# Second MLP of a three-stage kernel: out2's matmuls in rows of four instead of six, and one product of val moved on VectorE

## The chip, the cores and the metric

The kernel runs on one core of one Trainium2 chip, as one launch. The metric is the device time of that launch in microseconds (us), the median of several runs; less is better. The core has the engines TensorE (PE for matmuls, PEld for the weight loads that go ahead of them), VectorE (DVE), ScalarE (ACT) and GpSimd (POOL), and SyncE (SP), from which the transfers are started.

## What is computed

The reference computes an attention whose scores are masked by hash buckets, and two MLPs behind it. The second MLP, on 1536 tokens with a width of 512 and a hidden width of 1536, is what the change touches:

```python
def _moe2_ref(x, w_gate, w_val, w_out):
    g = x @ w_gate
    silu = g * (1.0 / (1.0 + np.exp(-g)))
    val = x @ w_val
    return (silu * val @ w_out).astype(np.float32)
```

## The kernel before

All matmuls run in fp32r with every operand split into a high and a low part, and a product is three matmuls: high x high, high x low, low x high (`each_of_three`, L802).

The second MLP runs in twelve steps, m = 0 to 11: two halves of the tokens (768 each) times six pairs of chunks of the hidden width. A step has a gate group and a val group (`group`, L1125) and is followed by its share of out2, which the next step carries. A group forms a 256 x 768 block by a scheme of seven half-size products in place of eight. Each of the seven is six matmuls of 384 columns into a PSUM bank; here they are named by bank and product: X1, Y6, X2, Y7, Z5, Y4, Z3, in this order. There are two banks only. X and Z share one, Y is the other, and the next group takes them the other way round: its X lies where this group's Y was, its Y where this group's Z was.

Between the products DVE and ACT read the banks. The ACT copies X1 to p1 (L1156). DVE forms u2 = p1 + Y6 (L1148); the next product into that bank, Y7, can't start before DVE has read it. In the same way u3 = p1 + Y7 stands ahead of Y4, the sum of Z5 ahead of Z3, the sum of Y4 ahead of the next group's X1, and the sum of Z3, which is the group's last addition, ahead of the next group's Y6. The four results are the quarters "11", "22", "21", "12".

In a gate group each quarter goes through Silu on ACT (tile sg, L1097). In a val group each quarter is multiplied by sg on DVE (L1103, `gating`, tile u), then copied by ACT to its high part uh (L1108), and DVE forms the low part ul = u - uh (L1109, both in `two`). Three of the four products read one operand from PSUM; that of "22" reads two SBUF tiles (val and sg). It is not issued at once but put on a list, `later`, and so is every `two`. `settle(n)` issues the first n entries of that list. So `settle` decides where on the queues of DVE and ACT these stand, and both engines work through their queues in order.

out2 of step m is 36 matmuls of 512 columns (tile o): the quarters in the order "11", "22", "21", "12", nine matmuls each. They need uh and ul of their quarter. They are handed out by a generator, `filler`, a few at each of the seven places `rest(0)` to `rest(6)` behind the products of the next step's groups. `counts` says how many at each place; before the change steps 2 to 11 have (6, 0, 6, 0, 6, 0, 0) in gate and (0, 6, 0, 6, 0, 6, 0) in val. out2 of the last step, m = 11, has no groups behind it and runs at the end in the order "11", "21", "22", "12".

`prepare` (L1035) makes the weight pieces of the coming group out of two loaded chunks: sums and differences x and y on DVE (L1057 to L1064, two SBUF operands each), high parts on ACT and low parts on POOL (L1030, L1031, tiles gate_t and val_t). `chores(k)` puts a part of it behind each product. In steps 1 to 5 `token_sums` for the second half of the tokens runs there too (L979, L987, L1004, L1006), and in step 6 the first half's results are copied out of PSUM (L1241, L1243, tile ot). The fill of the list by step is the same on every engine: the order is written out by hand, and no planner moves it.

Of the kernel before, what the change touches and what calls it, by code (L numbers as in the profile page):

```python
# [27 lines left out]
def lsh_attention_moe_moe2(  # L28
# [1096 lines left out]
    def group(nm, m, filler, counts, chores):  # L1125


        g = 2 * m + (nm == "val")
        sb, p = divmod(m, NPP)
        (pa, ta), (pb, tb_) = banks[g % 2], banks[1 - g % 2]  # L1130
        w = pieces.pop((nm, m))
        rights = {
            i: (quarter(xh, kh, th, sb), quarter(xl, kh, th, sb))
            for i, kh, th in ((1, 0, 0), (2, 1, 0), (3, 1, 1))
        }
        def temp(what):
            return pools["right"].tile([P, HALF], F32, tag="w", bufs=NR, name=f"{nm}{m}{what}")

        def mm(bank, i, first):
            right = rights[i] if i < 4 else sums_of_x[sb, {4: 3, 5: 0, 6: 1, 7: 2}[i]]  # L1140
            product(bank, w[i], right, first)

        def rest(k):
            for _ in range(counts[k]):
                next(filler, None)

        def add(out, a, bank):
            nc.vector.tensor_tensor(out=out, in0=bank[:, :HALF], in1=a, op=ALU.add)  # L1148
            return out

        X = pa.tile([P, 512], F32, tag=ta, name=f"{nm}{m}X")
        Y = pb.tile([P, 512], F32, tag=tb_, name=f"{nm}{m}Y")
        mm(X, 1, True)
        rest(0)
        p1 = temp("p1")
        nc.scalar.activation(out=p1, in_=X[:, :HALF], func=AF.Copy)  # L1156
        settle(2)
        late = nm == "gate" and m in (0, NPP)
        if not late:
            chores(0)  # L1160
        mm(Y, 6, True)
        rest(1)
        u2 = add(temp("u2"), p1, Y)
        if late:
            chores(0)
        chores(1)
        mm(X, 2, False)
        rest(2)
        take(nm, m, "11", X[:, :HALF])
        chores(2)  # L1170
        mm(Y, 7, False)
        rest(3)
        u3 = add(temp("u3"), p1, Y)
        settle(1)
        chores(3)
        Z = pa.tile([P, 512], F32, tag=ta, name=f"{nm}{m}Z")
        mm(Z, 5, True)
        rest(4)
        take(nm, m, "22", add(temp("22"), u3, Z))
        chores(4)  # L1180
        mm(Y, 4, False)
        rest(5)
        take(nm, m, "21", add(temp("21") if nm == "gate" else Y[:, :HALF], p1, Y))
        settle(1)
        chores(5)
        mm(Z, 3, False)
        rest(6)
        take(nm, m, "12", add(temp("12") if nm == "gate" else Z[:, :HALF], u2, Z))
        settle(1)
        chores(6)  # L1190

    out_v = out.rearrange("(b p c) d -> b c p d", b=B, c=NBLK)
# [119 lines left out]
    for m in range(NSTEP):  # L1312
        if m == 0:
            ahead = out2(0)
            filler = itertools.chain(out1(N1 - 2), out1(N1 - 1), ahead)
        else:
            filler = ahead if m == 1 else out2(m - 1)
        if m == 1:
            tsum = token_sums(
                1,  # L1320
                lambda i, name: (early if i % 2 else pools["late"]).tile(
                    [P, 2, HALF], F32, tag="raw", bufs=2, name=name
                ),
            )
        for nm in ("gate", "val"):
            nxt = ("val", m) if nm == "gate" else ("gate", m + 1)
            after = ("gate", m + 1) if nm == "gate" else ("val", m + 1)
            ready = prepare(*nxt)

            def chores(k):  # L1330
                if k == 0:
                    fetch_group(*after)
                next(ready, None)
                rows = {("val", 0, 0): [0], ("val", 0, 2): [1], ("val", 0, 3): [2], ("val", 0, 5): [3]}
                out1_close(N1 - 1, rows.get((nm, m, k), []))
                if nm == "gate" and k == 3:
                    fetch2("out2", m, 0)
                    fetch2("out2", m, 1)
                if nm == "val" and k in (1, 3):
                    prepare_out(m, 0 if k == 1 else 1)  # L1340
                if 1 <= m < 5 and k in (2, 5):
                    next(tsum, None)
                if m == NPP - 1 and nm == "val" and k in (2, 4, 5, 6):
                    next(tsum, None)

            if m == 0:
                counts = (2, 2, 2, 2, 2, 3, 3) if nm == "gate" else (2, 2, 2, 2, 0, 2, 2)
            elif m == 1 and nm == "gate":
                counts = (6, 0, 4, 0, 4, 0, 0)
            else:  # L1350
                counts = (6, 0, 6, 0, 6, 0, 0) if nm == "gate" else (0, 6, 0, 6, 0, 6, 0)
            group(nm, m, filler, counts, chores)
            for _ in ready:
                pass
        for _ in filler if m else ():
            pass
# [34 lines left out]
```

## Time and profile before

| | |
|---|---|
| median of 3 runs | 770.41 us (770.36 to 770.46) |
| the profiled execution | 770.41 us, span 768.5 us |
| PE busy | 761.5 us (99%), 4107 matmuls |
| PEld busy | 640.1 us (83%) |
| DVE busy | 547.9 us (71%) |
| ACT busy | 520.8 us (68%) |
| POOL busy | 487.2 us (63%) |
| the chain that ended last | PE 97%, ACT 1%, DVE 1% |
| second MLP's steps | from about 481 us to 764 us |

The page gives busy time by engine and the chain of work that ended last, followed back from the last instruction. A matmul's record starts when it starts, and its end is modelled and reaches over the start of the next one; so the pace is read from the starts, and a stall from a start that comes late or from a wait of PEld, which loads the weights just ahead. Where the timeline merges equal instructions, the row gives the first start, the time to the last end, and the count.

### The profile page before, as it was taken

How to read it: one execution, taken by the hardware profiler on the slowest of the kernel's cores; microseconds unless marked ns; L12 is line 12 of the kernel's file. 1: busy time of each engine (PE TensorE's matmuls, PEld its weight loads, DVE VectorE, ACT ScalarE, POOL GpSimd, SP SyncE). 2: the span in 40 equal slices, each digit the busy share in tenths (PEclk: the TensorE clock that was granted, in tenths of full speed). 3: DMA queues.
4: the chain of work that ended last, by engine and by line, in shares of the span. 5: the costliest groups of instructions: out<-in, count | busy, mean ns of one | idle time of the engine just before them, and what ended most of it. 6: DMA issues, size and time to landing. Idle time of an engine off the chain costs nothing.

```text
span 768.5 us, 12675 instructions
## 1 busy us (share of the span) xinstructions
PE 761.5 (99%) x4107; PEld 640.1 (83%) x4107; DVE 547.9 (71%) x1092; ACT 520.8 (68%) x1020; POOL 487.2 (63%) x424
## 2 busy tenths in 40 slices
PE   8999999999999999999999999999999999999998
PEld 5777868777777888888888888999999999999996
DVE  7777778777755787766666798587776787665553
ACT  7778887988878788887788777653444454444433
POOL 5647555554556776777778988666665595656450
PEclk9999999999999999999999999999999999999999
DMA  7577576757115777688866755122222215221102
GB/s 217 135 180 165 164 191 150 202 164 179 56 55 174 243 261 255 205 309 285 280 186 217 239 175 185 42 70 82 70 54 72 69 27 205 70 82 43 42 1 83
DMA packets 72692, 113.01 MB, mean 147 GB/s; under 512 B 6675, under 2 KB 44979, under 8 KB 72627
## 3 DMA queue, kind: packets, MB, share of 16 engines
q1 hardware_dynamic: 72352, 112.08, 48.7%
q8 instruction: 33, 0.54, 0.3%
q14 instruction: 33, 0.26, 0.1%
q10 hardware_dynamic: 274, 0.13, 0.1%
HBM read 76.29 MB, written 18.35 MB: 123 GB/s over the span
## 4 chain that ended last, share of the span: by engine, by line
PE 97%; ACT 1%; DVE 1%; issue 0%; POOL 0%; DVEq 0%
PE o L804 30%; PE h L804 17%; PE av L618 8%; PE t L600 8%; PE s L540 4%; PE s L543 4%; PE pj L341 1%; PE trk L285 1%; PE trq L285 1%; ACT p L561 1%; PE gate6Y L804 0%; PE gate7Y L804 0%; PE gate0Y L804 0%; PE val6Y L804 0%; PE val5Y L804 0%; PE val2Y L804 0%
## 5 line engine op out<-in xcount | busy, mean ns | idle before, releaser
L579 POOL TENSOR_SCALAR p<-p,rv 128x768 f32<-128x768 f32 x96 | 89.0, 944 | 68.3 <-DVE rv L572 61.6
L550 DVE TENSOR_SCALAR_CACHE_REDUCE p<-s 128x768 f32<-128x768 f32 x96 | 91.5, 955 | 26.7 <-PE s L543 10.6
L561 ACT ACTIVATE p<-p,mn 128x768 f32<-128x768 f32 x96 | 89.0, 934 | 2.9 <-DVE p L550 2.7
L606 ACT ACTIVATE pt<-t 128x384 f32<-128x384 f32 x140 | 63.9, 488 | 23.8 <-PE t L600 23.6
L600 PE MATMUL t<-ident,p 128*128 128x128 f32 x576 | 79.1, 274 | 0.6 <-POOL p L579 0.5
L600 PEld LDWEIGHTS t<-ident,p 128*128 128x128 f32 x576 | 66.8, 140 | 13.6 <-POOL p L579 6.2
L618 PE MATMUL av<-pt,vn 128*64 128x384 f32 x384 | 66.0, 491 | 0.0
L1108 ACT ACTIVATE uh<-u 128x384 fp32r<-128x384 f32 x48 | 23.8, 521 | 59.1 <-DVE u L1103 59.1
L835 DVE SCALAR_TENSOR_TENSOR rf<-ki,h 128x512 f32<-128x512 int32 x47 | 32.7, 696 | 39.3 <-ACT ki L832 39.3
L540 PE MATMUL s<-Y,X 128*128 128x384 f32 x192 | 57.6, 381 | 0.5 <-DVE p L550 0.3
L618 PEld LDWEIGHTS av<-pt,vn 128*64 128x64 f32 x384 | 26.2, 137 | 34.9 <-issue 34.7
L847 ACT ACTIVATE r<-r 128x512 f32<-128x512 f32 x48 | 30.3, 632 | 31.1 <-DVE r L839 30.9
L859 DVE TENSOR_TENSOR g<-h,r 128x512 f32<-128x512 f32 x48 | 33.0, 687 | 24.6 <-ACT r L848 24.0
L543 PE MATMUL s<-W,Z 76*128 76x384 f32 x192 | 49.4, 339 | 0.7 <-DVE Z L469 0.5
L1097 ACT ACTIVATE sg<-gate 128x384 f32<-128x384 f32 x36 | 18.9, 525 | 43.0 <-DVE gate L1148 42.9
L139 ACT ACTIVATE w<-raw 128x512 f32<-128x512 f32 x68 | 44.9, 662 | 2.0 <-DMA raw<-in_moe_w_in_dram 2.0
L804 PE MATMUL o<-out_1s,uh 128*128 128x512 f32 x144 | 45.0, 392 | 0.0
L804 PE MATMUL o<-out_0s,uh 128*128 128x512 f32 x142 | 44.3, 392 | 0.0
L155 DVE TENSOR_SCALAR bw<-w 128x512 int32<-128x512 int32 x55 | 37.8, 688 | 3.2 <-ACT w L139 2.0
L832 ACT ACTIVATE ki<-h 128x512 int32<-128x512 f32 x48 | 28.3, 590 | 14.9 <-PE h L804 14.8
L160 DVE SCALAR_TENSOR_TENSOR w<-raw,bw 128x512 int32<-128x512 int32 x55 | 37.3, 679 | 0.3
L848 ACT ACTIVATE r<-r,halfpi 128x512 f32<-128x512 f32 x48 | 34.8, 725 | 1.5
(1824 smaller groups left out, 2389.4 us busy)
## 6 DMA issues: line engine op xcount, KB each, us to landing
f<-w SPq DMA_DIRECT2D x58, 256.0 KB
raw<-in_moe_w_out_dram SPq DMA_DIRECT2D x28, 512.0 KB
raw<-in_moe_w_in_dram SPq DMA_DIRECT2D x16, 512.0 KB
raw<-in_moe_w_gate_dram SPq DMA_DIRECT2D x12, 512.0 KB
raw<-in_moe_w_val_dram SPq DMA_DIRECT2D x12, 512.0 KB
Y<-kH SPq DMA_DIRECT2D x28, 192.0 KB
vn<-in_v_dram SPq DMA_DIRECT2D x8, 384.0 KB
gate_0f<-f SPq DMA_DIRECT2D x12, 256.0 KB
```

Source lines behind the costliest of these rows:

```text
L139: nc.scalar.activation(out=t, in_=raws[i][:, :, 1].bitcast(F32), func=AF.Prelu, scale=2.0**-112, alpha=-(2.0**32),)
L155: nc.vector.tensor_scalar(out=word, in0=ti, scalar1=3, scalar2=None, op0=ALU.logical_shift_left)
L160: nc.vector.scalar_tensor_tensor(out=ti, in0=low, scalar=29, in1=word, op0=ALU.logical_shift_right, op1=ALU.bitwise_or)
L540: nc.tensor.matmul(out=ps[:, e, :HALF], lhsT=X[:, j, qs], rhs=Y[:, j, ks], start=True, stop=False)
L543: nc.tensor.matmul(out=ps[:, e, :HALF], lhsT=Z[:KZ, j, qs], rhs=W[:KZ, j, ks], start=False, stop=True)
L550: nc.vector.tensor_scalar(out=pt.rearrange("p (e s) -> p e s", e=2), in0=ps[:, :, :HALF], scalar1=-MASKED, scalar2=None, op0=ALU.min, op1= ...
L561: nc.scalar.activation(out=pt, in_=pt, func=AF.Exp, bias=nbias.pop((u, j)), scale=-1.0, accum_out=sums[u][:, j : j + 1],)
L579: nc.gpsimd.tensor_scalar(out=pt, in0=pt, scalar1=rv[:, j : j + 1], scalar2=1.0, op0=ALU.mult, op1=ALU.mult)
L600: nc.tensor.transpose(ps[:, c * P : (c + 1) * P], src[:, kb * P : (kb + 1) * P], ident)
L606: nc.scalar.activation(out=o, in_=s3, func=AF.Copy)
L618: nc.tensor.matmul(out=ps[j * D : (j + 1) * D, :HALF], lhsT=nat["v", pr][:, j, BLOCKS[kb], :], rhs=pts[half, j][:, kb, :], start=(kb == 0) ...
L804: nc.tensor.matmul(out=out_ap, lhsT=s, rhs=m, start=first and i == 0, stop=last and i == 2, **flags)
```

## The change

The change does two things in the second MLP. The counts: steps 2 to 11 now have nine rows of four out2 matmuls, five in the gate group and four in the val group, in place of six rows of six; steps 0 and 1 are regrouped to rows of four in the same way, with the same sums per step. And the order on DVE in a val group: the `settle(1)` behind the quarter "21" is dropped, and the last one settles two entries. So the product of "22" (`gating`) stands behind val's last addition and the product of "12", and its `two` follows it.

```diff
@@ -1181,12 +1181,13 @@
         take(nm, m, "21", add(temp("21") if nm == "gate" else Y[:, :HALF], p1, Y))
-        settle(1)
+        if nm == "gate":
+            settle(1)
         chores(5)
         mm(Z, 3, False)
         rest(6)
         take(nm, m, "12", add(temp("12") if nm == "gate" else Z[:, :HALF], u2, Z))
-        settle(1)
+        settle(1 if nm == "gate" else 2)
         chores(6)
@@ -1344,11 +1345,11 @@
             if m == 0:
-                counts = (2, 2, 2, 2, 2, 3, 3) if nm == "gate" else (2, 2, 2, 2, 0, 2, 2)
-            elif m == 1 and nm == "gate":
-                counts = (6, 0, 4, 0, 4, 0, 0)
+                counts = (4, 0, 4, 0, 4, 0, 4) if nm == "gate" else (2, 2, 2, 2, 0, 2, 2)
+            elif m == 1:
+                counts = (4, 0, 4, 4, 0, 0, 4) if nm == "gate" else (0, 4, 0, 4, 0, 4, 4)
             else:
-                counts = (6, 0, 6, 0, 6, 0, 0) if nm == "gate" else (0, 6, 0, 6, 0, 6, 0)
+                counts = (4, 4, 0, 4, 4, 0, 4) if nm == "gate" else (4, 0, 4, 4, 0, 4, 0)
```

On DVE, the passage from val of step 8 to gate of step 9. First the order before: u_22 is the product of two SBUF tiles, val8Z the last addition, ul the low parts, gate9u the sum u2 that Y7 waits for.

```order
L1103 TENSOR_TENSOR u_21_8139<-val8Y,sg_21_8026 128x384
L1103 TENSOR_TENSOR u_22_8123<-val_8121,sg_22_8014 128x384
L1148 TENSOR_TENSOR val8Z<-val8Z,val8u_8075 128x384
L1103 TENSOR_TENSOR u_12_8151<-val8Z,sg_12_8038 128x384
L1109 TENSOR_TENSOR ul_22_8154<-u_22_8123,uh_22_8153 128x384
L1109 TENSOR_TENSOR ul_21_8175<-u_21_8139,uh_21_8174 128x384
L1109 TENSOR_TENSOR ul_12_8179<-u_12_8151,uh_12_8178 128x384
L1057 TENSOR_TENSOR val9y<-val_1f 128x256
L1148 TENSOR_TENSOR gate9u_8200<-gate9Y,gate9p_8172 128x384
```

The product stood ahead of the last addition. Now the same passage of the changed kernel:

```order
L1103 TENSOR_TENSOR u_21_8139<-val8Y,sg_21_8024 128x384
L1148 TENSOR_TENSOR val8Z<-val8Z,val8u_8075 128x384
L1103 TENSOR_TENSOR u_12_8150<-val8Z,sg_12_8040 128x384
L1103 TENSOR_TENSOR u_22_8125<-val_8123,sg_22_8012 128x384
L1109 TENSOR_TENSOR ul_22_8154<-u_22_8125,uh_22_8153 128x384
L1109 TENSOR_TENSOR ul_21_8173<-u_21_8139,uh_21_8172 128x384
L1109 TENSOR_TENSOR ul_12_8177<-u_12_8150,uh_12_8176 128x384
L1057 TENSOR_TENSOR val9y<-val_1f 128x256
L1148 TENSOR_TENSOR gate9u_8202<-gate9Y,gate9p_8170 128x384
```

The product is now the third row behind the one that it stood behind, with the last addition and the product of "12" ahead of it; the three ul, val9y and gate9u follow in the order they had.

On PE, the gate group of step 9 from the end of Y6 to the start of Y7, before (gate9X is X2, o is out2):

```order
L804 MATMUL gate9Y<-T2h_7345,gate9t_8058 128x384
L804 MATMUL gate9X<-xh,gate9t_8057 128x384
L804 MATMUL gate9X<-xl,gate9t_8057 128x384
L804 MATMUL gate9X<-xh,gate9t_8057 128x384 x2
L804 MATMUL gate9X<-xl,gate9t_8057 128x384
L804 MATMUL gate9X<-xh,gate9t_8057 128x384
L804 MATMUL o_1_2_7694<-out_8_0s,uh_11_8105 128x512 x2
L804 MATMUL o_1_2_7694<-out_8_0s,ul_11_8106 128x512
L804 MATMUL o_1_3_7695<-out_8_1s,uh_22_8153 128x512 x2
L804 MATMUL o_1_3_7695<-out_8_1s,ul_22_8154 128x512
L804 MATMUL gate9Y<-T3h_7385,gate9t_8058 128x384
```

Six matmuls of out2 stood between X2 and Y7. In the changed kernel:

```order
L804 MATMUL gate9Y<-T2h_7349,gate9t_8064 128x384
L804 MATMUL o_1_1_7693<-out_8_0s,uh_11_8107 128x512
L804 MATMUL o_1_1_7693<-out_8_0s,ul_11_8108 128x512
L804 MATMUL o_1_2_7694<-out_8_0s,uh_11_8107 128x512 x2
L804 MATMUL gate9X<-xh,gate9t_8063 128x384
L804 MATMUL gate9X<-xl,gate9t_8063 128x384
L804 MATMUL gate9X<-xh,gate9t_8063 128x384 x2
L804 MATMUL gate9X<-xl,gate9t_8063 128x384
L804 MATMUL gate9X<-xh,gate9t_8063 128x384
L804 MATMUL gate9Y<-T3h_7387,gate9t_8064 128x384
```

Four matmuls of out2 now stand between Y6 and X2, and Y7 follows X2 directly; the row ahead of Y6 went from six to four as well.

On DVE at the end, val of step 11, before (val11Z is the last addition, and nothing but out2 of step 11 follows on PE):

```order
L1103 TENSOR_TENSOR u_21_8818<-val11Y,sg_21_8724 128x384
L1103 TENSOR_TENSOR u_22_8804<-val_8802,sg_22_8712 128x384
L1148 TENSOR_TENSOR val11Z<-val11Z,val11u_8786 128x384
L1103 TENSOR_TENSOR u_12_8828<-val11Z,sg_12_8736 128x384
L1109 TENSOR_TENSOR ul_22_8831<-u_22_8804,uh_22_8830 128x384
```

And in the changed kernel:

```order
L1103 TENSOR_TENSOR u_21_8818<-val11Y,sg_21_8722 128x384
L1148 TENSOR_TENSOR val11Z<-val11Z,val11u_8761 128x384
L1103 TENSOR_TENSOR u_12_8827<-val11Z,sg_12_8738 128x384
L1103 TENSOR_TENSOR u_22_8806<-val_8804,sg_22_8710 128x384
L1109 TENSOR_TENSOR ul_22_8831<-u_22_8806,uh_22_8830 128x384
```

The move is the same as in step 8. On ACT the order is unchanged at both places: uh of "22", then in step 8 the copy p1 of gate 9's X1, then uh of "21" and uh of "12".

## Rows read from the trace of the kernel before

**Rows 1.** Windows: stretch, us, busy PE, PEld, DVE, ACT, POOL (instructions), clock, DMA, GB/s
```profile
481.00:764.00 283.00, 282.93 (x1471) 261.68 (x1470) 190.58 (x326) 130.75 (x257) 167.58 (x137) 1.00 0.21 66
```
**Rows 2.** Waits of PEld, 480 to 769 us: total us, times, longest
```profile
PEld val0Z L804 <- DVE val L1148: 0.5, 1, 0.5
PEld gate6Y L804 <- DVE gate6u L1148: 0.4, 1, 0.4
PEld gate7Y L804 <- DVE gate7u L1148: 0.3, 1, 0.3
```
**Rows 3.** The chain that ended last, in order of time: start, us, what
```profile
540.17 1.39 PE o L804 x6
541.56 1.04 PE val2X L804 x6
...
677.27 1.06 PE val8Y L804 x6
```
**Rows 4.** Timeline, PE: first matmul of gate 9's X1: start, us, instruction
```profile
687.55 0.33 PE L804 MATMUL gate9X<-xh,gate9t 128*128 128x384 f32 x1
```
**Rows 5.** Timeline, DVE, val 8 to gate 9 (idle before and releaser in brackets)
```profile
686.39 0.97 DVE L1103 TENSOR_TENSOR u<-val,sg 128x384 f32<-128x384 f32 x1
687.75 0.56 DVE L1148 TENSOR_TENSOR val8Z<-val8Z,val8u 128x384 f32<-128x384 f32 x1 [0.39 <-PE val8Z L804]
688.35 0.56 DVE L1103 TENSOR_TENSOR u<-val8Z,sg 128x384 f32<-128x384 f32 x1
688.82 0.55 DVE L1109 TENSOR_TENSOR ul<-u,uh 128x384 fp32r<-128x384 f32 x1
689.78 1.02 DVE L1109 TENSOR_TENSOR ul<-u,uh 128x384 fp32r<-128x384 f32 x2 [0.41 <-ACT uh L1108]
690.73 0.42 DVE L1057 TENSOR_TENSOR val9y<-val_1f 128x256 f32<-128x256 f32 x1
691.29 0.56 DVE L1148 TENSOR_TENSOR gate9u<-gate9Y,gate9p 128x384 f32<-128x384 f32 x1
```
**Rows 6.** Timeline, ACT, the same passage
```profile
687.39 0.53 ACT L1108 ACTIVATE uh<-u 128x384 fp32r<-128x384 f32 x1 [3.09 <-DVE u L1103]
688.85 0.49 ACT L1156 ACTIVATE gate9p<-gate9X 128x384 f32<-128x384 f32 x1 [0.93 <-PE gate9X L804]
689.24 0.93 ACT L1108 ACTIVATE uh<-u 128x384 fp32r<-128x384 f32 x2
690.06 0.62 ACT L1030 ACTIVATE val9t<-val_0f 128x512 fp32r<-128x512 f32 x1
```
**Rows 7.** Timeline, POOL, the same passage
```profile
686.90 1.06 POOL L1031 TENSOR_TENSOR gate9t<-gate_1f,gate9t 128x256 fp32r<-128x256 f32 x1
690.76 1.54 POOL L1031 TENSOR_TENSOR val9t<-val_0f,val9t 128x512 fp32r<-128x512 f32 x1 [2.80 <-ACT val9t L1030]
```
**Rows 8.** Timeline, DVE, gate 7: the piece y, then u2, ahead of Y7
```profile
646.49 0.41 DVE L1057 TENSOR_TENSOR val7y<-val_1f 128x256 f32<-128x256 f32 x1
646.83 0.54 DVE L1148 TENSOR_TENSOR gate7u<-gate7Y,gate7p 128x384 f32<-128x384 f32 x1
```
**Rows 9.** Timeline, PE: the first two matmuls of gate 7's Y7
```profile
647.42 0.45 PE L804 MATMUL gate7Y<-T3h,gate7t 128*128 128x384 f32 x1
647.71 0.34 PE L804 MATMUL gate7Y<-T3l,gate7t 128*128 128x384 f32 x1
```
**Rows 10.** Timeline, DVE, val 5 to gate 6: the three ul
```profile
619.50 4.22 DVE L1109 TENSOR_TENSOR ul<-u,uh 128x384 fp32r<-128x384 f32 x3
```
**Rows 11.** Timeline, DVE, gate 4: the piece y
```profile
575.62 1.51 DVE L1057 TENSOR_TENSOR val4y<-val_1f 128x256 f32<-128x256 f32 x1
```
**Rows 12.** Timeline, POOL, gate 4: the low part that runs beside it
```profile
575.53 1.31 POOL L1031 TENSOR_TENSOR val4t<-val_0f,val4t 128x512 fp32r<-128x512 f32 x1 [1.19 <-ACT val4t L1030]
```
**Rows 13.** Timeline, PE, out2 of step 11: its first matmul, and the first of "21"
```profile
756.35 0.63 PE L804 MATMUL o<-out_0s,uh 128*128 128x512 f32 x2
758.43 0.62 PE L804 MATMUL o<-out_1s,uh 128*128 128x512 f32 x2
```

## The prediction

> **What bounds the kernel now.** I read the windows of the second MLP first: in the 283.00 us from 481 to 764 the PE is busy for 282.93 [rows 1]. Then the waits of the weight loads, since a stall can hide behind a modelled matmul end: in this whole stretch there are three, 0.5, 0.4 and 0.3 us long [rows 2]. Last the chain: six matmuls of out2 take 1.39 us, six of a product 1.04 [rows 3], that is 0.232 and 0.174 each, the same time per column (0.00045 us), so the grouping alone changes no matmul's pace. One product in the chain takes 1.06, Y6 of a val group, and so it is in most steps: 0.02 lost. So the stage is bound by a PE that hardly waits. All that a better order could win is 1.2 + 10 x 0.02 = 1.4 us at most, 0.18% of 770.4. A measurement of this kernel tells about 0.2% (1.54 us) from no change. A loss has no such limit: any wait that comes to stand ahead of a product lengthens the time by its full size.
>
> **The rows of four.** No matmul is added or taken away (36 of out2 a step either way). What changes is the cover, the PE work that runs while DVE reads a bank. I count it for each bank in steps 2 to 11. Before, two reads at the passage from gate to val had one product (1.04) as cover, which just does: the addition begins 0.20 after the last matmul (687.75 against the 687.55 at which the next product starts [rows 4, 5]) and takes 0.56. Afterwards nearly every read has one product and one row of four, 1.04 + 0.93 = 1.97. This takes away the 0.02 per step: 10 x 0.02 = 0.2 us won. The other side is the gate's first half. From the end of val's Z3 to the start of gate's Y7 stood X1, 6, Y6, X2, 6: 3 x 1.04 + 2 x 1.39 = 5.91 us. Now it is X1, 4, Y6, 4, X2: 3 x 1.04 + 2 x 0.93 = 4.98. That is 0.93 us less for the longest chain of the step, the next part.
>
> **The moved product.** It stands now behind the last addition and the product of "12". Who waits for it: on ACT uh of "22", and in its queue behind it p1, uh of "21" and uh of "12"; on DVE ul of "22", and behind it the two other ul, the piece y, and then u2, which Y7 waits for. Before, the product ended 0.19 before Z3 did (686.39 + 0.97 = 687.36 against 687.55 [rows 4, 5]), so ACT had uh of "22" done early (687.39 [rows 6]) and p1 started as soon as X1 was there, at 688.85, 1.30 after Z3's end.
>
> I count from Z3's end. The addition starts at +0.20, the product of "12" at +0.80 (688.35), the next DVE instruction at +1.27 (688.82 [rows 5]). That is now the moved product. For its length the trace has 0.97 in its old place, with POOL's piece beside it (686.90 to 687.96 [rows 7]), and 0.55 for the subtraction of the same size, also of two SBUF tiles, that ran at +1.27 with POOL idle [rows 5]. I take 0.55, since POOL's piece is over or nearly over by then. So it ends at +1.82, and ACT starts uh of "22" 0.03 later, as before, at +1.85. The ACT's next ones follow at the spacing of their rows (0.53 and 0.40 for the two uh, 0.39 from p1 to uh [rows 6]): p1 at +2.28, uh of "21" at +2.67, uh of "12" at +3.07 to +3.60. p1 is 0.98 later than before. On DVE ul of "21" starts as its uh ends, +3.21, ul of "12" at +3.68, y 0.48 later at +4.16 (689.78 to 690.73 is 0.95 for two [rows 5]), u2 0.34 after y where PE doesn't hold it [rows 8], +4.50, and takes 0.56: it ends at +5.06. From u2's end to a Y7 at full pace I have one case: u2 ended at 647.37, the second matmul of Y7 began at 647.71, one pace (0.17) behind a start at 647.54 [rows 8, 9], 0.17 after u2. So Y7 can start at +5.23, and its place is +4.98: **0.25 us of stall** for a passage of this kind. Before, the place was +5.91 and u2 was no limit.
>
> The Trainium skill, page "SBUF — State Buffer", section "Who interferes with whom", says that a DVE instruction with two SBUF inputs and a GpSimd instruction that reads SBUF exclude each other, and that the one which issues second waits for the whole of the first. The trace agrees in kind: the same form takes 0.55 alone and 0.97 beside POOL. By that rule the product has its short form at +1.27 only if POOL's piece is over; with 0.97 there instead, the stall would be 0.67 and the seven passages named below would cost 2.9 us more.
>
> **Passages one by one.** Steps 0 to 1 and 1 to 2 keep a row or half a row of out2 behind val's Z3 (counts 2 and 4 at the last place), which gives the chain 0.46 and 0.93 us back: no stall. Steps 7 to 11, four passages like the one above: 4 x 0.25 = 1.0. Steps 2 to 5, three passages with token sums on POOL: the piece y took 1.51 there in place of 0.42, since it was issued just behind POOL's low part (575.62 against 575.53 [rows 11, 12]). With y slow, Y7 waits 1.09 more, 1.34; with y fast 0.25. I take 0.5, nearer to the fast end, since now the ul of "22" comes later and no longer meets the POOL piece that delayed it: 1.5. Step 5 to 6: POOL runs without a break, and three ul took 4.22, 1.41 each [rows 10]; Y7 waited already [rows 2]. One more instruction of two SBUF tiles in this queue is 1.41, the cover is 0.93 shorter: 2.3 (low end 0.93 + 0.25 = 1.2, if the product finds a gap between POOL's pieces; high end 2.3 + 1.09 = 3.4, if y too meets a piece). Step 6 to 7: copies of results stand in the queue, Y7 waited already [rows 2]; 0.98 for the later chain and 0.93 of cover: 1.9 (low end 0.9, the cover alone; high end 1.9 + 1.09 = 3.0).
>
> **The end.** out2 of step 11 takes "11", then "21" 2.08 us later (756.35 to 758.43 [rows 13]). Before, the PE didn't wait there: 2.08 is nine times 0.23. Now, without a p1 between, ACT does uh of "22" at +1.85 and uh of "21" at +2.28 to +2.81, and the matmul can follow 0.17 later, +2.98: a stall of **0.9 us**, with nothing behind it that could take it up.
>
> **The other queues.** The transfers of SP keep their order but for one result block of step 6, which goes two places earlier; the weight pieces lead by more than a shift of 1 us on POOL takes away: the last one of gate 9 was done at 687.96 [rows 7], and its first matmul, Y4, stood five products and three rows of out2 behind Z3's end, 5 x 1.04 + 3 x 1.39 = 9.4 us. These edits I put at nothing; the cover is that lead.
>
> Sum: 1.0 + 1.5 + 2.3 + 1.9 + 0.9 - 0.2 = 7.4. The profiled execution has 770.41 us, the median too (span 768.5), so **777.8 us**.
>
> **The rivals.**
> - **A: the seven ordinary passages are covered.** The 0.25 is a difference of 5.23 and 4.98. If two or three of the spacings are 0.1 shorter, it is gone, and with y always fast in steps 2 to 5 nothing is left there. Then 2.3 + 1.9 + 0.9 - 0.2 = 4.9: 775.3 us, and with the low ends of steps 5 to 7 it is 1.2 + 0.9 + 0.9 - 0.2 = 2.8, 773.2 us. For it: the margin is thin. Against it: each spacing is from a row and recurs in each step.
> - **B: y meets POOL in every passage.** In step 9 y was issued at 690.73 and POOL's low part at 690.76 [rows 5, 7], 0.03 apart, both hanging on uh of "12". If y loses, Y7 waits 1.09 more: 7 x 1.34 + 4.9 = 14.3, 784.7 us. Against it: the distance between the two chains behind uh of "12" is not altered. By the rule of the Trainium skill named above, the second of the two waits for all of the first, so that this is decided by hundredths; the 1.51 of rows 11 agrees.
> - **C: not slower.** The product leaves the time in which POOL is busy, DVE and POOL stop holding each other up, and the larger cover of the gate's second half takes away the stalls on record, so that Y7 is reached in time everywhere. This decides at one point: u2 has to end by +4.81. Then the time is 770.4 - 0.2 and less what Y7 lost in gates 6 and 7, at most 0.4 + 0.3 [rows 2]: 769.5 to 770.2 us, I take 769.9; and the end must not lose its 0.9 either, so uh of "21" would have to be done by +1.9. Against it: the product can't be issued before +1.27, and three ACT instructions follow in order.
>
> **How the numbers follow.** Forecast 777.8 (own range 774.9 to 780.3: steps 2 to 5 at 0.25 and steps 5 to 7 at their low ends, or steps 2 to 5 at 1.34 each): 0.52. A: 0.22. B: 0.15. C: 0.11, of it 0.04 for more than I can account for, faster by over 0.2%. The range from 772.5 to 784.0 holds the forecast's, A's with 0.7 to spare below for the end's term, and the lower half of B's, where y loses only here and there; C and the rest of B stay out, about 0.19. Faster by over 0.2%: 0.04; within 0.2%: 0.10 (C and the lowest of A); slower: 0.86.
>
> **What would show it.** In the changed profile: PEld waits for DVE at gateY in steps 2 to 11 (the addition of u2, L1148), largest at gate6Y and gate7Y; the ACT's p1 in gate groups starts about 2.3 after Z3's end and not 1.3; PEld or PE of o waits for ACT uh once behind val11. The waits of val's Y6 are gone. I am wrong if the gateY waits are missing (A or C), if y shows 1.5 us in steps 7 to 10 (B), or if products wait on banks or weight pieces that I counted as covered: val's u3 ahead of Y4, the quarter "21" ahead of the next X1.

## The result, and the profile after the change

The changed kernel takes 777.67 us (median of five runs, 777.45 to 777.98), the kernel before 770.36 in the same comparison. The ratio is 1.0097, with a 95% interval of 1.0082 to 1.0112: slower by about 1%, far outside the 0.2% that this kernel's measurement can't tell from no change. The forecast was 777.8. The profiled execution took 777.85 us, its span 776.0, against 770.41 and 768.5 before.

The changed kernel's page, the busy times (columns: busy us, share of the span, instructions):

```profile
PE 763.8 (98%) x4107; PEld 638.7 (82%) x4107; DVE 548.1 (71%) x1092; ACT 520.1 (67%) x1020; POOL 485.9 (63%) x424
```

No engine has more to do, and the matmuls are as many. So the 7.4 us are waits. The window that answers to [rows 1], on the changed kernel:

```profile
481.00:771.40 290.40, 285.61 (x1469) 260.69 (x1468) 190.33 (x326) 129.50 (x257) 165.76 (x137) 1.00 0.20 64
```

PE is busy for 285.61 of 290.40 us, where it was busy for all but 0.07. Where it waits is read from PEld, as in [rows 2] (waited for: us in total, times, longest); [rows 2] had three lines, and here stand the longest and a sample of the rest:

```profile
PEld gate6Y L804 <- DVE gate6u L1148: 1.7, 1, 1.7
PEld gate7Y L804 <- DVE gate7u L1148: 1.6, 1, 1.6
PEld val6Z L804 <- DVE val L1148: 1.5, 1, 1.5
PEld o L804 <- ACT uh L1108: 1.0, 1, 1.0
PEld gate5Y L804 <- DVE gate5u L1148: 0.7, 1, 0.7
...
PEld gate1Y L804 <- DVE gate1u L1148: 0.5, 1, 0.5
...
PEld gate9Y L804 <- DVE gate9u L1148: 0.3, 1, 0.3
```

The weights are loaded a little ahead, so these figures are 0.1 to 0.2 above what PE itself loses. What PE loses I read from the starts of its matmuls: a matmul of 384 columns is followed by the next after 0.174 us, one of 512 after 0.232; what is beyond that is lost. An example, gate 9's Y7 in the changed kernel (columns: start, us, instruction):

```profile
698.13 0.34 PE L804 MATMUL gate9X<-xh,gate9t 128*128 128x384 f32 x1
698.42 0.44 PE L804 MATMUL gate9Y<-T3h,gate9t 128*128 128x384 f32 x1
698.70 0.34 PE L804 MATMUL gate9Y<-T3l,gate9t 128*128 128x384 f32 x1
```

From 698.13 to 698.42 are 0.29, and to the next 0.28: 0.12 + 0.11 = 0.23 us lost, half by waiting and half by starting again. All such gaps above 0.05 us in the second MLP add up to 8.75 us after the change and to 0.78 before. The difference, 7.97, less the 0.15 of val's Y6 (below), is 7.8; from the first matmul of gate 0 to the last of out2 it is 7.7 (482.58 to 772.03 against 482.75 to 764.50).

The passage from val 8 to gate 9 is the one that the prediction counted through. DVE (to compare with [rows 5]; val8Z's last matmul gives way to gate 9's X1 at 693.33):

```profile
693.53 0.57 DVE L1148 TENSOR_TENSOR val8Z<-val8Z,val8u 128x384 f32<-128x384 f32 x1 [0.57 <-PE val8Z L804]
694.13 0.56 DVE L1103 TENSOR_TENSOR u<-val8Z,sg 128x384 f32<-128x384 f32 x1
694.60 0.55 DVE L1103 TENSOR_TENSOR u<-val,sg 128x384 f32<-128x384 f32 x1
695.74 0.56 DVE L1109 TENSOR_TENSOR ul<-u,uh 128x384 fp32r<-128x384 f32 x1 [0.59 <-ACT uh L1108]
696.53 1.03 DVE L1109 TENSOR_TENSOR ul<-u,uh 128x384 fp32r<-128x384 f32 x2 [0.23 <-ACT uh L1108]
697.48 0.42 DVE L1057 TENSOR_TENSOR val9y<-val_1f 128x256 f32<-128x256 f32 x1
697.81 0.55 DVE L1148 TENSOR_TENSOR gate9u<-gate9Y,gate9p 128x384 f32<-128x384 f32 x1
```

and ACT (to compare with [rows 6]):

```profile
695.18 0.52 ACT L1108 ACTIVATE uh<-u 128x384 fp32r<-128x384 f32 x1 [2.73 <-DVE u L1103]
695.61 0.48 ACT L1156 ACTIVATE gate9p<-gate9X 128x384 f32<-128x384 f32 x1
695.99 0.93 ACT L1108 ACTIVATE uh<-u 128x384 fp32r<-128x384 f32 x2
```

Measured from 693.33 the product stands at +1.27 and takes 0.55, uh of "22" stands at +1.85, p1 at +2.28, the next uh at +2.66, y at +4.15 and u2 at +4.48. Each is within 0.02 of the prediction's list. Y7 runs at full pace from +5.20 on (698.70 less one pace of 0.17), 0.23 late.

### The profile page after: what moved, and what is told of

It reads as the page before. It is cut to its first block, busy times and chain, and to the rows that moved or that the text cites. A ratio compares the mean times of both kernels' runs of the same rounds, so it can differ in the third digit from the quotient of the medians.

```text
span 776.0 us, 12668 instructions
## 1 busy us (share of the span) xinstructions
PE 763.8 (98%) x4107; PEld 638.7 (82%) x4107; DVE 548.1 (71%) x1092; ACT 520.1 (67%) x1020; POOL 485.9 (63%) x424
## 5 line engine op out<-in xcount | busy, mean ns | idle before, releaser
L804 PE MATMUL o<-out_0s,uh 128*128 128x512 f32 x142 | 47.7, 392 | 0.0
L804 PE MATMUL o<-out_1s,uh 128*128 128x512 f32 x144 | 46.8, 394 | 0.6 <-ACT uh L1108 0.6
L543 PEld LDWEIGHTS s<-W,Z 76*128 76x128 f32 x192 | 34.8, 189 | 1.7 <-ACT W L466 1.7
```

What stands on the lines that cost most here:

```text
L543: nc.tensor.matmul(out=ps[:, e, :HALF], lhsT=Z[:KZ, j, qs], rhs=W[:KZ, j, ks], start=False, stop=True)
L804: nc.tensor.matmul(out=out_ap, lhsT=s, rhs=m, start=first and i == 0, stop=last and i == 2, **flags)
```

## The experiments

All are compared with runs of the kernel before on the same chip, 770.09 to 770.32 us; the runs stand on three chips, so two of them are set beside each other by their ratios and by what they lose. "Lost" is what PE loses, read as above. The changed kernel loses 8.75.

**1. The rows alone.** The new counts, with the product where it was:

```diff
-        if nm == "gate":
-            settle(1)
+        settle(1)
...
-        settle(1 if nm == "gate" else 2)
+        settle(1)
```

> Rows of four as in the changed kernel, the product of "22" back ahead of val's last addition. Theory 1 (the moved product keeps ACT and so u2 back; the rows only take away cover): u2 then ends some 4.1 us after Z3 against a place of 4.98, so no wait at gateY in steps 2 to 4 and 7 to 11, and no wait at the end; what is left is the 1.3 us wait at val6Z, which the rows brought by moving the copies of results: 771 to 772 us. Rival 2 (the new places of the rows cost by themselves, through banks and POOL): the gateY waits stay, 775 us or more.

Measured 776.52 us (776.43 to 776.60), ratio 1.0081 (1.0065 to 1.0097), 7.3 lost. The expectation is wrong: most of the whole loss is there with the rows alone. Of it 1.3 stands ahead of val 6's Z3, 1.9 ahead of Y6 in gates 3, 4, 5 and 9, 3.4 ahead of Y7 in gates 1 and 3 to 7, and 0.4 at val 0, as before the change. DVE in this run, from val 8 to gate 9 (gate 9's X1 starts at 693.43):

```profile
692.97 1.37 DVE L1103 TENSOR_TENSOR u<-val,sg 128x384 f32<-128x384 f32 x1
694.27 0.55 DVE L1148 TENSOR_TENSOR val8Z<-val8Z,val8u 128x384 f32<-128x384 f32 x1
694.86 0.56 DVE L1103 TENSOR_TENSOR u<-val8Z,sg 128x384 f32<-128x384 f32 x1
```

and POOL beside it:

```profile
692.65 1.28 POOL L1031 TENSOR_TENSOR gate9t<-gate9y,gate9t 128x512 fp32r<-128x512 f32 x1
```

The product starts 0.46 before Z3's last matmul gives way, where it was 1.16 before [rows 4, 5]; 0.46 of the difference are the two matmuls that the row between Y4 and Z3 has less (in gates 8, 10 and 11 it starts 0.69 before). It falls into POOL's piece, takes 1.37 and holds back val's last addition, which starts at +0.84 and not at +0.20. The product of "12", which also reads that bank, ends at 695.42, and Y6 of gate 9 starts at 695.56, 0.24 late. Y6 of gates 3 and 4 loses 0.24 too and Y6 of gate 5 1.2. So the regrouping isn't neutral: it puts the product of two SBUF tiles where POOL is busy. That explains the 1.9 at Y6, not the whole. At Y7 the cover is shorter, by 0.93 (0.5 in gate 1): in gates 1 and 7 u2 ends 5.27 and 5.83 us behind Z3 in this run, 5.26 and 5.85 in the kernel before, where the longer cover hid all of it but 0.1 in gate 7. In gates 3 to 5 the late product comes on top (u2 ends at 5.75, 5.74 and 6.25, before at 5.25, 5.27 and 5.33).

**2. The move alone.** The product behind val's last addition, with the counts of before:

```diff
-                counts = (4, 4, 0, 4, 4, 0, 4) if nm == "gate" else (4, 0, 4, 4, 0, 4, 0)
+                counts = (6, 0, 6, 0, 6, 0, 0) if nm == "gate" else (0, 6, 0, 6, 0, 6, 0)
```

(and steps 0 and 1 likewise.)

> The product moved as in the changed kernel, the rows of six as before. Theory 1: the ordinary passages have 5.91 us of cover for a chain of 5.2, so no wait at gateY in steps 8 to 11; the late passages (steps 3 to 7) wait about 0.3 to 0.6 each, and the end waits its full 1.05 us: 772 to 774 us. Rival 2: only the rows cost, so 770.4 and a few tenths.

Measured 775.54 us (775.15 to 775.75), ratio 1.0068 (1.0052 to 1.0084), above the expected range; 6.3 lost: 1.1 at the end, 1.8 in gate 6 (X2 and Y7 0.9 each) and 0.9 in gate 7 where 0.3 to 0.6 each were expected, 0.6 behind val 0, and 0.3 at val 0's Z3, as before the change. Gates 8 to 11 lose nothing, as the cover of 5.91 us says. The rest, 0.5 at each Y6 of val 2, 3 and 4, was not expected. At val 2, DVE:

```profile
538.07 1.23 DVE L987 TENSOR_TENSOR x<-x,x 128x384 f32<-128x384 f32 x1
539.23 0.54 DVE L1148 TENSOR_TENSOR gate<-gate2Z,gate2u 128x384 f32<-128x384 f32 x1
```

The subtraction of token sums, two SBUF tiles, runs beside POOL here and takes 1.23 (0.55 in the kernel before), and the gate's last addition behind it comes too late for Y6, which in the old rows has one product as cover.

Apart the two halves lose 7.3 and 6.3, run together 8.75. They don't add up. In part the traces show why: the moved product leaves the place where the new rows hurt it (with both, Y6 of gates 3, 4 and 9 loses nothing and that of gate 5 0.16, where the rows alone lose 0.24 each and 1.2), and the new rows give Y6 of val 2 to 4 the cover that it lacks above (it loses nothing).

**3. uh of "22" last.** The changed kernel with the high and low parts of "22" issued behind those of "21" and "12", so that on ACT p1 comes ahead of all three uh:

```diff
-        settle(2)
+        settle(3)
...
-        settle(1 if nm == "gate" else 2)
+        settle(1)
+        if nm == "val":
+            later.append(later.pop(0))
...
-    settle(2)
+    settle(3)
```

> The changed kernel, but the high and low part of "22" are issued after those of "21" and "12"; the product itself stays behind the last addition. Theory 1 (ACT's queue is the path: uh of "22" stands ahead of p1 and of the other uh): p1 starts again 1.3 us after Z3, u2 ends about 4.5 after it, so the waits at gateY of steps 8 to 11 and the wait at the end go: 771.5 to 773.5 us, with the val6Z wait left. Rival 3 (the product's own time on DVE is the path): u2 moves by less than 0.2 us and the waits stay, 776 us or more.

Measured 775.41 us (775.19 to 775.59), ratio 1.0067 (1.0051 to 1.0083), 6.1 lost. The mechanism holds: gates 8 to 11, gate 1, gate 7 and the end lose nothing at all. In gate 9 (X1 at 692.56), ACT's p1 and DVE's u2:

```profile
693.86 0.49 ACT L1156 ACTIVATE gate9p<-gate9X 128x384 f32<-128x384 f32 x1 [2.14 <-PE gate9X L804]
```

```profile
696.55 0.55 DVE L1148 TENSOR_TENSOR gate9u<-gate9Y,gate9p 128x384 f32<-128x384 f32 x1
```

p1 is at +1.30, as before the change, and u2 at +3.99 instead of +4.48. But the total missed the expectation: gates 5 and 6 still lose 0.87 and 1.62, and gates 3 and 4 now lose 0.94 each (0.33 before this edit). In gate 3, DVE's y and POOL's low part:

```profile
553.04 1.51 DVE L1057 TENSOR_TENSOR val3y<-val_1f 128x256 f32<-128x256 f32 x1
```

```profile
552.89 1.37 POOL L1031 TENSOR_TENSOR val3t<-val_0f,val3t 128x512 fp32r<-128x512 f32 x1 [1.13 <-ACT val3t L1030]
```

y was issued 0.15 behind POOL's piece and took 1.51. In the changed kernel it is 0.03 ahead of it and takes 0.42. That is rival B's mechanism, let in by the new order on DVE.

**4. The old order in the last step only.** The changed kernel, with the product of step 11 in its old place:

```diff
-        if nm == "gate":
+        if nm == "gate" or m == NSTEP - 1:
             settle(1)
...
-        settle(1 if nm == "gate" else 2)
+        settle(1 if nm == "gate" or m == NSTEP - 1 else 2)
```

> The changed kernel, with the old place of the product in the last step alone. Theory 1: the wait of out2's matmul for uh behind the last step goes, with nothing behind it that takes it up: 1.0 us less than the changed kernel, 776.6 us. If the end is bounded by the copies and the output transfer and not by this wait: 777.7 us.

Measured 776.45 us (776.14 to 776.81), ratio 1.0079 (1.0061 to 1.0097). That is 1.2 less than the changed kernel's 777.67, but the two ratios' intervals overlap; what shows the term is the trace. The waits of o for uh and ul, 1.05 lost, are gone from it, and all others are as they were, within 0.04. The end is a term of its own.

**5 and 6. Less cover and more.** The changed kernel with two matmuls of out2 in the gate group moved behind Y7, or ahead of it:

```diff
-                counts = (4, 4, 0, 4, 4, 0, 4) if nm == "gate" else (4, 0, 4, 4, 0, 4, 0)
+                counts = (4, 2, 0, 6, 4, 0, 4) if nm == "gate" else (4, 0, 4, 4, 0, 4, 0)
```

```diff
-                counts = (4, 4, 0, 4, 4, 0, 4) if nm == "gate" else (4, 0, 4, 4, 0, 4, 0)
+                counts = (4, 4, 2, 2, 4, 0, 4) if nm == "gate" else (4, 0, 4, 4, 0, 4, 0)
```

> The changed kernel with one difference: in steps 2 to 11 two of the four out2 matmuls between Y6 and X2 of a gate group go behind Y7 instead. The cover from Z3's end to Y7 becomes 4.52 us in place of 4.98. Theory (Y7 waits for a chain that ends at a fixed distance, about 5.2, from Z3): each Y7 that already waits does so 0.46 longer: gates 8 to 11 from 0.23 to 0.69 each, gates 3 to 5 from about 0.4 to 0.9, gate 6 from 1.6 to 2.1, gate 7 from 1.5 to 2.0; nine passages x 0.46 = 4.2, so 781.8 us. Rival (the wait hangs on something that moves with PE, as POOL's pieces or the reading of the bank): the waits stay within 0.1 of what they were, 777.2 to 778.5 us.

> The changed kernel with one difference: in steps 2 to 11 two of the four out2 matmuls behind Y7 of a gate group go ahead of it. The cover from Z3's end to Y7 becomes 5.44 us in place of 4.98, above the 5.2 at which the chain is done. Theory: Y7 of gates 8 to 11 loses 0 in place of 0.23, gates 3 and 4 lose 0 in place of 0.33, gates 5, 6 and 7 each lose 0.46 less (0.6 to 0.15, 1.6 to 1.2, 1.5 to 1.05), what stands elsewhere stays: 2.96 less, 774.7 us. Rival (DVE's queue follows PE, so that u2 gets later with the cover; or the two matmuls that then lack behind Y7 make Z5 or Y4 wait for DVE): Y7's waits fall by less than half of that, or new waits appear at Z5 or Y4, 776 to 778 us.

Measured 781.68 us (781.36 to 782.51), ratio 1.0152 (1.0137 to 1.0167), and 775.06 us (774.85 to 775.48), ratio 1.0063 (1.0046 to 1.0080). PEld's wait in gate 9 with less cover:

```profile
PEld gate9Y L804 <- DVE gate9u L1148: 0.7, 1, 0.7
```

With less, gates 8 to 11 lose 0.66 each instead of 0.23, gates 3 and 4 0.75 instead of 0.33, gate 5 1.06 instead of 0.61, gate 7 1.94 instead of 1.51, gate 6 1.89 instead of 1.62 and another 0.19 at X2. With more, gates 3, 4 and 8 to 11 lose nothing, and gates 5, 6 and 7 0.1, 1.2 and 1.05. In both directions each passage moves by what its cover moved, or to zero. In gates 8 to 11 u2 ends 5.03 us behind Z3 in all three kernels: the chain's end doesn't depend on where these two matmuls stand. These are the runs that carry the prediction's main step.

**7. Copies on ACT.** In step 6 the changed kernel copies the first half's results out of PSUM on ACT and DVE by turns. Here all on ACT:

```diff
-        if s % 2 == 0 or sb == B - 1:
+        if True:
```

> The changed kernel, but in step 6 all copies of the first half's results run on ACT, where half of them ran on DVE. Theory (the copy on DVE ahead of u3 in val 6 shifts the three DVE instructions behind it into POOL's pieces): the wait ahead of val 6's Z3, 1.30, falls to under 0.3, and gate 7's Y7 from 1.51 to something between 0.25 and 1.4; 775.0 to 776.5 us. Rival (the wait comes from the rows of four alone, with the copy of no account): val 6's Z3 keeps 1.0 or more, 777 to 778 us; the longer queue on ACT may then add to it.

Measured 775.98 us (775.65 to 776.34), ratio 1.0076 (1.0061 to 1.0091). The wait ahead of val 6's Z3 is gone, and gate 7 loses 0.97 instead of 1.51. In the changed kernel a copy of results stands there between the ul on DVE, so that the piece y comes 0.24 behind POOL's piece; DVE and POOL:

```profile
650.06 1.51 DVE L1057 TENSOR_TENSOR val7y<-val_1f 128x256 f32<-128x256 f32 x1
```

```profile
649.82 1.47 POOL L1031 TENSOR_TENSOR val7t<-val_0f,val7t 128x512 fp32r<-128x512 f32 x1 [3.10 <-ACT val7t L1030]
```

With the copies on ACT y takes 0.42 (at 649.01, 0.04 ahead of POOL's piece). The 0.97 that are left are 0.23 as in gates 8 to 11, 0.26 for the product, which takes 0.81 beside POOL, and 0.49 by which the last two ul wait longer for ACT, 0.72 us and not 0.23.

In the changed kernel DVE had, in val 6:

```profile
639.97 0.69 DVE L1244 COPY ot<-o 128x512 f32<-128x512 f32 x1 [0.48 <-PE o L804]
640.58 0.55 DVE L1148 TENSOR_TENSOR val6u<-val6Y,val6p 128x384 f32<-128x384 f32 x1
641.04 1.46 DVE L1109 TENSOR_TENSOR ul<-u,uh 128x384 fp32r<-128x384 f32 x1
642.43 1.50 DVE L1064 TENSOR_TENSOR gate7y<-gate_0f,gate7x 128x256 f32<-128x256 f32 x1
643.86 0.55 DVE L1148 TENSOR_TENSOR val<-val6Z,val6u 128x384 f32<-128x384 f32 x1
```

and POOL:

```profile
640.80 1.30 POOL L1031 TENSOR_TENSOR out_1s<-out_1f,out_1s 128x512 fp32r<-128x512 f32 x1 [1.59 <-ACT out_1s L1030]
642.05 1.60 POOL L1031 TENSOR_TENSOR gate7t<-gate7x,gate7t 128x512 fp32r<-128x512 f32 x1
```

With the copies on ACT, DVE has there:

```profile
640.91 0.56 DVE L1109 TENSOR_TENSOR ul<-u,uh 128x384 fp32r<-128x384 f32 x1 [0.94 <-ACT uh L1108]
641.39 0.42 DVE L1064 TENSOR_TENSOR gate7y<-gate_0f,gate7x 128x256 f32<-128x256 f32 x1
641.72 0.55 DVE L1148 TENSOR_TENSOR val<-val6Z,val6u 128x384 f32<-128x384 f32 x1
```

In the changed kernel ul and the piece y run into two POOL pieces, take 2.96 in place of 0.98, and Z3 starts 1.3 late. The new rows move both sides of this meeting. On DVE a second copy of results stands ahead of u3 in val 6, which before the change stood behind the sum of Z5. On ACT a copy comes earlier, and with it the high part that POOL waits for: POOL's piece starts 0.57 us behind Z5's first matmul (640.23), before the change 1.70 (638.70 against 637.00). Run 7 takes the meeting away from POOL's side: ul starts where it did (640.91 and 641.04), and POOL's first piece at 642.00 and not at 640.80, since ACT has one more copy ahead of its high part. So the run shows that the meeting makes the wait; which of the two moved copies brings it about is not shown.

**8. Token sums on DVE.** The changed kernel with the second half's token sums, additions and low parts, on DVE instead of POOL:

```diff
-                nc.gpsimd.tensor_tensor(
+                (nc.vector if sb else nc.gpsimd).tensor_tensor(
...
-                (nc.gpsimd if sb else nc.vector).tensor_tensor(
+                nc.vector.tensor_tensor(
```

> The changed kernel, but the token sums' additions and low parts for the second half of the tokens run on DVE, where they ran on POOL. Theory (in steps 2 to 6 it is POOL's pieces that stretch the product, the ul and y): Y7 of gates 3 to 5 falls from 0.33, 0.32 and 0.61 to the 0.25 of gates 8 to 11, gate 6 from 1.62 to under 1.0; 776 to 777 us. Rival (it is the length of DVE's queue that counts, whoever else runs): DVE has more to do in these steps, and the waits there grow: 778 to 782 us, with new ones ahead of val's products.

Measured 782.72 us (782.33 to 782.87), ratio 1.0162 (1.0145 to 1.0179). The theory's forecast fell, and the time lies a little above the rival's range: gates 3 and 4 lose 0.75 and 0.78 (0.33 and 0.32 with the sums on POOL) and gate 5 the same as before this edit, 0.78, Y6 and Y7 together. Ahead of val's products hardly a new wait came (0.2 us of PEld at val 5's Z3). An addition of token sums now stands on DVE ahead of val's last one (1.53 us at 549.00, beside a POOL piece for the weights), so that this starts late. So it is still POOL that stretches DVE's instruction: the run shows that taking the sums off POOL doesn't help, not that POOL's pieces are of no account. The first matmul of gate 6 comes 3.3 us late, and the trace gives as its releaser only "issue": on DVE low parts of the sums (2.31 us at 620.60, after a wait for ACT's high part) stand ahead of the addition that this X1 waits for. The run does not show what the steps would cost if nobody had the sums; that was not tried.

**9. Rows in val alone.** The kernel before, with the rows of val groups alone changed, so that Y6 gets more cover:

```diff
-                counts = (6, 0, 6, 0, 6, 0, 0) if nm == "gate" else (0, 6, 0, 6, 0, 6, 0)
+                counts = (6, 0, 6, 0, 6, 0, 0) if nm == "gate" else (4, 2, 0, 6, 0, 6, 0)
```

> The kernel before with one difference: in val groups of steps 2 to 11 the six out2 matmuls behind Y6 are split, four behind X1 and two behind Y6. The gate groups and the passages into them are as before. Theory (the only thing to win is the 0.02 at val's Y6, and only the passage into the gate is sensitive): the 10 x 0.02 are gone and no wait is new: 770.1 us. Rival (any shift of the rows against POOL's pieces costs, as the run with the new counts alone seemed to say): new waits in val groups of steps 2 to 6, 771 to 774 us.

Measured 770.48 us (769.79 to 771.08) beside 770.09 of before, ratio 1.0005 (0.9996 to 1.0014). It can't be told from no change, in either direction. In its trace 1.04 us are lost in all, 0.25 of it new, at gate 5's Y6.

**10. All four remedies.** The changed kernel with the additional cover of run 6, the copies of run 7, and the product in its old place in steps 5 and 11:

```diff
-        if nm == "gate":
+        if nm == "gate" or m in (5, NSTEP - 1):
             settle(1)
...
-        settle(1 if nm == "gate" else 2)
+        settle(1 if nm == "gate" or m in (5, NSTEP - 1) else 2)
...
-        if s % 2 == 0 or sb == B - 1:
+        if True:
...
-                counts = (4, 4, 0, 4, 4, 0, 4) if nm == "gate" else (4, 0, 4, 4, 0, 4, 0)
+                counts = (4, 4, 2, 2, 4, 0, 4) if nm == "gate" else (4, 0, 4, 4, 0, 4, 0)
```

> The changed kernel with all that the runs showed to take a wait away: the cover of 5.44 us as in the run with two matmuls more ahead of Y7, the copies of step 6 all on ACT, and the product in its old place in steps 5 and 11. Theory (the waits are separate and add up): what stays is val 0's Z3 with 0.35, gate 1 with 0.5, gate 5 with 0.3, gate 6 with 0.2 and gate 7 with 0.5, 1.9 in all, where the changed kernel lost 8.75: 770.4 to 771.5 us, the time of the kernel before within what a measurement tells. Rival (they are coupled through POOL and DVE, as the two halves of the change are: 6.2 and 5.2 us apart, 7.3 together): taking one away lets another come, 772 to 774 us.

Measured 770.76 us (770.18 to 771.10) beside 770.32 of before, ratio 1.0006 (0.9997 to 1.0016); 1.35 lost instead of 8.75. With these edits what is left of the change costs nothing that can be told. It brings nothing either. The product's old place in step 5 was not run by itself. The 0.5 less than expected is gate 1, whose loss is gone though no edit touches it (last section). The longest that is left of PEld's waits:

```profile
PEld gate7Y L804 <- DVE gate7u L1148: 0.7, 1, 0.7
```

No version tried is faster than the kernel before.

## Why the prediction was right, and where it was not

The main step was right, and the runs show it. That the time was hit to 0.1 us (777.8 against 777.67) is luck: two terms were too large and two places were missed, and these errors took each other up. What PE loses more than before, by the prediction's terms:

| term | predicted, us | measured, us |
|---|---|---|
| rows of four, val's Y6 | -0.2 | -0.15 |
| steps 7 to 11, Y7 of gates 8 to 11 | 1.0 | 0.9 |
| steps 2 to 5, gates 3 to 5 | 1.5 | 1.43 |
| step 5 to 6, gate 6 | 2.3 | 1.3 |
| step 6 to 7, gate 7 | 1.9 | 1.4 |
| the end | 0.9 | 1.05 |
| gate 1 | 0 | 0.49 |
| val 6, ahead of Z3 | not named | 1.30 |
| sum | 7.4 | 7.7 |

(The time grew by 7.44 between the profiled executions; before gate 0 and behind out2 the changed one gains the difference.)

**The moved product and the ordinary passages: right.** ACT's queue carries the delay from the product to p1 and y to u2, and u2 ends at +5.03 by its row, where 5.06 was counted. Runs 5 and 6 show that Y7's place against that fixed end makes the wait, and run 3 that it is uh of "22" ahead of p1 that sets it. By these, rival A (the 0.25 vanishes) and C (not slower) are out. In the changed kernel y wins against POOL by 0.03 us in gate 9, as it did before the change; rival B didn't come in these passages, but run 3 shows that it lay that close, and in gate 7 y lost (below).

**Steps 2 to 5: the size is luck.** The 0.5 for each passage was a value between a fast y (0.25) and a slow one (1.34). In the changed kernel y is fast in all three, 0.42. Gates 3 and 4 lose 0.33 and 0.32, since the product takes 0.64 there, beside POOL, and not 0.55. Gate 5 loses 0.61 at Y7 and 0.16 at Y6 for a reason that the prediction doesn't name: a subtraction of token sums on DVE stands ahead of val's last addition and takes 1.54 beside POOL, so that the addition starts at +0.77:

```profile
595.31 1.54 DVE L987 TENSOR_TENSOR x<-x,x 128x384 f32<-128x384 f32 x1
```

Before the change the addition was as late (+0.88), and the longer row hid it. This is read from the traces; no run takes that subtraction away.

**The end: right.** The stall ahead of "21" and the three short ones behind it are 1.05; run 4 takes them away.

**Step 5 to 6: over-sized.** The prediction put in one more instruction at 1.41, on the high side of its bounds. In the changed kernel the product found the gap that the low bound named. DVE and POOL:

```profile
621.00 0.55 DVE L1103 TENSOR_TENSOR u<-val,sg 128x384 f32<-128x384 f32 x1
```

```profile
621.07 1.64 POOL L1031 TENSOR_TENSOR gate6t<-gate6y,gate6t 128x512 fp32r<-128x512 f32 x1
```

The product took 0.55, and POOL's piece was the one that got longer, 1.64 where the like took 1.30. From Z3's end to u2's end the queue took 5.96 before (618.22 to 624.18) and 6.43 after (619.73 to 626.16): 0.47 more, not 1.41. That is the sum of both halves: with the rows alone (run 1) u2 ends 5.47 behind Z3, 0.49 earlier than before the change, since the first ul takes 0.87 and not 1.64, and the move adds 0.96 to that. With the 0.93 of cover the 0.47 are the 1.4 that Y7 lost more; 0.1 came back at gate 6's Z5. The high end of the term, a slow y, couldn't come: in gate 6 y stands behind u2, in the kernel before too.

**Step 6 to 7: over-sized.** The prediction added the ordinary passage's delay of p1, 0.98, to the lost cover. But before the change it was not ACT that set this passage: the ul met POOL's pieces there (1.14 and 1.64 for two of the three). From Z3's end to u2's end were 5.85 us (641.52 to 647.37), and 6.40 after (645.63 to 652.03): 0.55 more, not 0.98. After the change the ul are fast (0.55 each), and the 6.40 are the 5.03 of an ordinary passage, 0.28 for the copy of results and 1.09 for y, which loses to POOL's piece (1.51, rows at run 7). So rival B's mechanism came in this one passage, as the high end of the term has it, and stayed unseen in the sum, since the delay that it was to be added to had mostly gone. With 0.93 of cover the 0.55 are about the 1.4 measured. So in both passages the failed step is the same: a delay that is added to a queue with waits of its own partly takes their place.

**Gate 1: missed.** The prediction gave this passage a surplus of cover and used the product's short form. In the trace the product takes 1.14 there, at POOL's side (rows in the last section), so p1 comes 0.6 later than in the one run where the product was short, and X2 and Y7 wait. The step "POOL's piece is over or nearly over by then" was taken from step 9 and not looked up for step 0.

**Val 6: missed.** The prediction named the copies of results only for the queue at the passage into gate 7, and costed the rows of four at nothing beside the cover. It should have followed, for the step in which out2 has consumers on DVE and ACT, where each copy stands in their queues once the rows move. The list of possible surprises had u3 ahead of Y4; what came was one product later, the sum of Z5 ahead of Z3.

**The rows alone: not foreseen.** The prediction put at nothing what the rows of four cost beside the cover. Run 1 shows that the rows alone cost 6.2 us: 1.9 by the product that runs into POOL's piece ahead of Y6, 1.3 at val 6, and most of the rest by the shorter cover. The move spares the first of these and has its own price.

The Trainium skill, page "SBUF — State Buffer", section "Who interferes with whom", was weighed in the prediction: a DVE instruction with two SBUF inputs and a GpSimd one that reads SBUF exclude each other, and the order of issue decides who waits. The runs agree: 0.42 against 1.51 for the same piece y, 0.55 against 1.37 for the same product, and 1.46 against 0.56 for ul. Of the order of issue the recorded starts tell it only where they lie far enough apart (last section).

## What to carry to other kernels

Where PE never waits, count for each bank the PE work between its last reader's start and its next writer, and set beside it the chain on the other engines, through every instruction that stands in order on their queues. A change of the order of the rows is not neutral on the other engines: it shifts each two-operand SBUF instruction against POOL's pieces and each copy of a result in DVE's queue, so follow these in every step that has a different queue, not in one. And a total that comes out right can hide terms that don't; the account by places is what shows it.

## What the runs showed of the hardware

**A tie of 0.01 us decides half a microsecond.** At the passage from val 0 to gate 1 the product and POOL's piece are issued together. DVE and POOL in the changed kernel:

```profile
505.08 1.14 DVE L1103 TENSOR_TENSOR u<-val,sg 128x384 f32<-128x384 f32 x1
```

```profile
505.07 0.73 POOL L1031 TENSOR_TENSOR gate1t<-gate_1f,gate1t 128x256 fp32r<-128x256 f32 x1
```

and with the four remedies, none of which touches this step:

```profile
505.24 0.55 DVE L1103 TENSOR_TENSOR u<-val,sg 128x384 f32<-128x384 f32 x1
```

```profile
505.23 1.17 POOL L1031 TENSOR_TENSOR gate1t<-gate_1f,gate1t 128x256 fp32r<-128x256 f32 x1
```

In one run DVE waits and POOL is short, in the other the reverse, at the same recorded distance; gate 1 loses 0.49 in the one and nothing in the other. Of the nine runs with the moved product eight have it long, with POOL's start recorded from 0.017 us ahead of DVE's to 0.008 behind it. Which of the two comes first can't be forecast from such rows. The piece y tells how far that reaches, for a POOL that was idle before: recorded 0.049 us or more behind POOL's start, y takes 1.5 (21 passages in all traces); recorded up to 0.040 behind it, as in gates 7 to 11 of run 3, y takes 0.42 and POOL's piece is the long one, 1.6.

**In run 8 PE stood still, and then its clock fell.** PE stood still from 620.9 to 624.1. The windows of that run (stretch, us, busy PE, PEld, DVE, ACT, POOL, clock, DMA share, GB/s):

```profile
620.90:624.10 3.20, 0.06 (x1) 0.01 (x1) 3.17 (x5) 0.70 (x1) 1.59 (x2) 1.00 0.00 0
624.10:625.30 1.20, 1.18 (x7) 1.20 (x8) 1.20 (x3) 0.00 (x0) 0.00 (x0) 1.00 0.00 0
625.30:628.50 3.20, 3.20 (x11) 2.82 (x10) 2.40 (x6) 2.03 (x5) 0.00 (x0) 0.50 0.00 0
```

The granted clock went to 0.50, the lower of its two levels (1.2 GHz), from 625.3 to 628.5, after PE had begun to work again, and then rose. A matmul of 384 columns took 0.32 from start to start there instead of 0.174, and 1.7 us were lost beyond the wait itself. The waits of the changed kernel, the longest 1.5 us, didn't lower it: around its two longest, from 620 to 632 and from 644 to 660, the granted clock is 1.00.
